# GpSimdE inverses, VectorE transposes of the small blocks, and two constant products ahead of each TensorE task of the first stage

## The chip, the cores and the metric

The kernel runs on one core of a Trainium2 chip. The metric is the device time of one execution in microseconds (us); a comparison uses medians of several runs. TensorE (PE in the profile) multiplies, VectorE (DVE), ScalarE (ACT) and GpSimdE (POOL) do elementwise work, and SyncE (SP) issues nearly all DMAs. TensorE's granted clock has two levels here, 1.2 and 2.4 GHz; the profile's PEclk gives their mean over a stretch, 0.5 and 1.0.

## The reference

A delta-rule attention over 4 batches, 8 heads, 768 steps and head size 48 feeds two feed-forward layers (width 384, hidden width 2048, 3072 tokens):

```python
for t in range(S):
    y[:, :, t] = q[:, :, t] @ state
    v_old = k_n[:, :, t] @ state
    state += beta[t] * outer(k_n[:, :, t], v[:, :, t] - v_old)
h = x @ w_in                       # first layer, rational function
P = a0 + a1*h + a2*h**2 + a3*h**3
Q = 1 + |b0|*|h| + |b1|*h**2
x = (P / (Q + 1e-6)) @ w_out
h = x @ w2_in                      # second layer
out = (max(h, 0)**2) @ w2_out
```

## The kernel before

The attention is cut into 12 chunks of 64 steps, and 4 batches of a chunk make 4 of its 48 sub-steps n (all heads at once). Within a chunk the recurrence is solved by the inverse of a triangular 64x64 matrix for each head, built from the Gram matrix of the keys. Eight sub-steps (two chunks) make a group g, of 0 to 5, whose inverses are made together.

**Inverses.** Tile Gb holds the 32x32 diagonal blocks of the Gram matrices, one block per partition, and Tt the inverses. For groups 2 to 5 the loop of L466 to L473 makes 31 steps of two VectorE operations each: a product into tmp (L471) and a subtraction into Tt (L472), of (s+1)(31-s) elements a partition (31 to 256), each depending on the one before. For groups 0 and 1 the loop of L457 to L465 inverts 16x16 blocks only, and products of TensorE on 32x32 blocks merge them: mA (L528) into E, mB (L540), mC (L552). For all groups m1 (L578) and m2 (L591) merge 32x32 blocks into 64x64 ones. ScalarE moves each result out of PSUM (L545, L557, L584, L596). Tt lies one block per partition, the products need blocks of rows: so Tt goes to DRAM (td) and comes back in four loads as TT, and its transpose (ScalarE's copy to Gb, L491) goes to DRAM (nd) and comes back as DN or TN.

**Sub-steps.** `first` computes K S and Q S (L666) and T v (also L666), `middle` copies and masks on ScalarE and GpSimdE (L699, L703), `rest` makes the outputs (L724, L725) and updates the state X on VectorE (L743). Outputs gather in xin, which `split` turns into xh and xl (L849, L850). Gram matrices of later groups (L425) go to DRAM in gs (L415).

**Feed-forward.** Layer 1 works in 6 tiles i of 512 tokens, each of 16 units j (128 hidden features): mm1 (9 products, L866) into a PSUM bank h, `rational` (L876 to L898), and mm2_1 (L904) some 15 us later. Tile i needs the two chunks of group i. Layer 2 follows with 96 units of mm1, relu2 and mm2_2 (L866, L915 to L930). There are three PSUM banks for h; a unit holds one until the last operation of `rational`, L895. In `rational` ScalarE copies h to SBUF (hs, L884), and GpSimdE makes b*a (L886), c = a3*hs + a2 (L887) and c*hs (L889).

**Order of work.** Nothing is ordered by hand. Every piece is a task with an engine, an estimated duration, a due time, and what it reads and writes; class Plan plays a list schedule of all tasks (`play`), moves due times by the result (`late`), repeats this 8 times and keeps the shortest. Each engine then executes its tasks strictly in that order, the DMAs of SP too. A task marked lock=1 on VectorE is never planned beside one marked so on GpSimdE. In `Plan.run`, gaps of over 0.6 us planned ahead of a TensorE task from 55 us before T0 = 88 us (planned start of layer 1) to 20 us after it are filled with products of a constant (128x128 by 128x256 bf16, L284), as many as 70% of the gap holds at 0.11 us each. They write a bank that is not read.

```python
for _ in range(int(0.7 * (gap - 0.2) / dur)):
    one()
```

## Time and profile before

| what | us |
|---|---|
| median of 3 runs | 1183.78 (1182.72 to 1186.74) |
| profiled execution, its own time | 1189.82 |
| its span, first to last instruction | 1188.1 |
| stage A, up to the first product of layer 1 | 113 |
| stage B, layer 1 with groups 1 to 5 of the attention | 113 to 785 |
| stage C, layer 2 | 785 to 1188 |

The page gives the busy time of each engine: PE 1088.5 us (92% of the span), DVE 716.0 (60%), ACT 676.3 (57%), POOL 459.2 (39%). These are means over three stages with different limits, so the profile is read by stage. In a row of the windows each engine has its busy time in us and, in brackets, its instructions. A row of the groups gives line, engine, operation, out<-in, shapes and count, then the busy time in us and the mean of one instruction in ns, then the idle time of the engine before them.

### The profile page before, as it was taken

The page shows a single profiled execution, that of the slowest core. Times are in us where ns is not written, and L with a number is a line of the kernel's source. Part 1 is how long each engine was busy: PE and PEld are TensorE (multiplying, and loading weights), DVE is VectorE, ACT ScalarE, POOL GpSimd, SP SyncE. Part 2 cuts the span into 40 slices and gives each one's busy share as a digit, 9 for nine tenths or more (in the row PEclk, how much of TensorE's full clock was granted, in tenths as well). Part 3 has the DMA queues.
Part 4 walks back from the last instruction along what each step waited for, and adds up shares of the span by engine and source line. Part 5 has one row for each costly group of instructions (what it writes and reads, how often), then busy time and mean ns, then how long its engine had stood idle before and what let it go on. Part 6 is the DMA issues. An engine that isn't in the chain of part 4 may idle for free.

```text
span 1188.1 us, 24846 instructions
## 1 busy us (share of the span) xinstructions
PE 1088.5 (92%) x10030; PEld 769.2 (65%) x10030; DVE 716.0 (60%) x1237; ACT 676.3 (57%) x1269; POOL 459.2 (39%) x479
## 2 busy tenths in 40 slices
PE   4687898799897998998899989999999999999998
PEld 4576565456554555655566646567788888888887
DVE  4353777887888689668755546788633343333432
ACT  5365876586667576765576867766523333243432
...
GB/s 223 175 186 162 85 65 144 142 152 40 84 80 126 15 86 87 109 9 59 54 81 17 20 83 80 33 154 138 67 9 27 27 18 36 1 27 1 27 1 27
DMA packets 135394, 87.83 MB, mean 74 GB/s; under 512 B 102384, under 2 KB 119920, under 8 KB 135280
## 3 DMA queue, kind: packets, MB, share of 16 engines
...
q14 instruction: 35, 0.29, 0.1%
...
## 4 chain that ended last, share of the span: by engine, by line
PE 72%; DVE 8%; issue 5%; DMA 4%; ACT 4%; POOL 3%; SPq 3%; ACTq 0%; POOLq 0%; DVEq 0%
PE bank L866 28%; PE bank L904 18%; PE bank L930 5%; PE bank L928 5%; PE bank L929 5%; PE bank L666 5%; SPq L316 3%; DVE tmp L471 2%; PE bank L724 2%; DVE Tt L472 2%; POOL A L825 1%; POOL C L832 1%; DMA kTg<-in_kS_dram 1%; DVE mem L893 1%; PE bank L578 1%
## 5 line engine op out<-in xcount | busy, mean ns | idle before, releaser
L866 PE MATMUL bank<-xh,A 128*128 128x512 f32 x1152 | 362.8, 396 | 3.6 <-POOL A L825 3.6
L904 PE MATMUL bank<-mem,B 128*128 128x512 f32 x576 | 289.0, 635 | 22.1 <-DVE mem L895 21.1
L866 PE MATMUL bank<-xl,A 128*128 128x512 f32 x576 | 258.7, 449 | 11.0 <-DVE mem L895 6.5
L866 PEld LDWEIGHTS bank<-xh,A 128*128 128x128 f32 x1152 | 219.9, 191 | 67.0 <-issue 15.1
L904 PEld LDWEIGHTS bank<-mem,B 128*128 128x128 f32 x576 | 107.6, 198 | 126.3 <-issue 88.7
L916 DVE SCALAR_TENSOR_TENSOR mem<-bank,mem 128x512 f32<-128x512 f32 x96 | 66.3, 691 | 152.2 <-ACT mem L915 152.1
L887 POOL TENSOR_SCALAR mem<-hs,par 128x512 f32<-128x512 f32 x96 | 79.6, 829 | 176.8 <-ACT hs L884 140.5
L866 PEld LDWEIGHTS bank<-xl,A 128*128 128x128 f32 x576 | 110.1, 191 | 54.3 <-issue 14.8
L915 ACT ACTIVATE mem<-bank 128x512 f32<-128x512 f32 x96 | 57.5, 599 | 152.2 <-PE bank L866 152.1
L886 POOL TENSOR_TENSOR mem<-mem 128x512 f32<-128x512 f32 x96 | 126.4, 1317 | 9.3 <-DVE mem L893 4.2
L889 POOL TENSOR_TENSOR mem<-mem,hs 128x512 f32<-128x512 f32 x96 | 125.4, 1306 | 7.4
L930 PE MATMUL bank<-gh,C 128*128 128x512 f32 x288 | 113.7, 395 | 0.0
L928 PE MATMUL bank<-gl,C 128*128 128x512 f32 x288 | 113.5, 394 | 0.0
L929 PE MATMUL bank<-gh,C 128*128 128x512 f32 x288 | 112.0, 389 | 0.0
L893 DVE SCALAR_TENSOR_TENSOR mem<-mem,par,bank 128x512 f32<-128x512 f32 x96 | 71.5, 745 | 61.0 <-ACT bank L892 60.6
L890 DVE SCALAR_TENSOR_TENSOR mem<-mem,par,bank 128x512 f32<-128x512 f32 x96 | 71.1, 741 | 59.4 <-POOL mem L889 56.0
L919 DVE TENSOR_TENSOR gl<-mem,gh 128x512 fp32r<-128x512 f32 x96 | 69.2, 722 | 60.0 <-ACT gh L918 60.0
L918 ACT CAST gh<-mem 128x512 fp32r<-128x512 f32 x96 | 59.6, 621 | 70.9 <-DVE mem L916 59.8
L883 ACT ACTIVATE mem<-bank 128x512 f32<-128x512 f32 x96 | 57.4, 598 | 73.2 <-PE bank L866 72.1
L891 ACT ACTIVATE mem<-mem,par 128x512 f32<-128x512 f32 x96 | 69.2, 721 | 29.2 <-POOL mem L886 28.5
L885 ACT ACTIVATE mem<-mem,par 128x512 f32<-128x512 f32 x96 | 78.5, 817 | 0.9
L703 POOL TENSOR_SCALAR_AFFINE_SELECT X<-X 64x256 f32<-64x256 f32 x96 | 42.0, 438 | 71.1 <-ACT X L699 64.4
(119 smaller groups left out, 1636.7 us busy)
## 6 DMA issues: line engine op xcount, KB each, us to landing
...
```

The lines of the kernel that those rows point to most:

```text
L866: M.matmul(h, a, b, start=(k == 0 and m == 0), stop=(k == NK - 1 and m == 2))
L885: add("ACT", 0.83, lambda: A_.activation(b(), a(), AF.Identity, bias=s(4), scale=s(5)), r=[ak, "par"], w=[bk], due=due + 3.8, alloc=(("b", ...
L886: add("POOL", 1.32, lambda: P_.tensor_tensor(b(), b(), a(), op=ALU.mult), r=[ak], w=[bk], due=due + 5, lock=1)
L887: add("POOL", 0.85, lambda: P_.tensor_scalar(c(), hs(), s(3), s(2), op0=ALU.mult, op1=ALU.add), r=[sk, "par"], w=[ck], due=due + 5, lock=1 ...
L889: add("POOL", 1.32, lambda: P_.tensor_tensor(c(), c(), hs(), op=ALU.mult), r=[sk], w=[ck], due=due + 6.5, lock=1, free=[sk])
L890: add("DVE", 0.775, lambda: V.scalar_tensor_tensor(c(), c(), s(1), h(), op0=ALU.add, op1=ALU.mult), r=[hk, "par"], w=[ck], due=due + 7.3)
L891: add("ACT", 0.72, lambda: A_.activation(a(), b(), AF.Ln, bias=s(6)), r=[bk, "par6"], w=[ak], due=due + 7)
L893: add("DVE", 0.775, lambda: V.scalar_tensor_tensor(c(), c(), s(0), h(), op0=ALU.add, op1=ALU.mult), r=[hk, "par"], w=[ck], due=due + 9)
L904: M.matmul(acc[d], Bw[j][:, 128 * d:128 * d + 128], slot[gk], start=(j == 0), stop=(j == NJ - 1))
L928: M.matmul(acc[d], wh, gl, start=(j == 0), stop=False)
L929: M.matmul(acc[d], wl, gh, start=False, stop=False)
L930: M.matmul(acc[d], wh, gh, start=False, stop=(j == NJ - 1))
```

## The change

Six edits come together. (1) The 31 inverse steps of groups 2 to 5 go from VectorE to GpSimdE. (2) `rational` drops the copy hs; c = a3*h + a2 is made by ScalarE out of PSUM, and h*c by VectorE. (3) For groups 0 and 1 two transposes on VectorE make Gb (the blocks of Tt, rows on partitions) and DN in place of the trips through td and nd; mA reads Gb instead of TT. (4) For group 0 the block N is made by ScalarE with a mask `half` instead of four DMAs; the copies `o2` go from ScalarE to VectorE. (5) `move`: for group 0, results at partitions 64 and above leave PSUM through VectorE, others through ScalarE as before, and each quarter is a task of its own. (6) Constant products: the window begins 64 us ahead of T0, gaps are filled by another formula, and each TensorE task planned from 58 us to 4 us ahead of T0 gets at least two. kTc has four buffers instead of three.

```diff
@@ -33,7 +33,7 @@
-ROUNDS = 8
+ROUNDS, FILL = 8, 2
...
-        lo, hi, one, dur = self.fill
+        lo, hi, one, dur, least = self.fill
         end = 0.0
         for i in self.order:
             if T[i]["eng"] == "PE":
                 gap = T[i]["s"] - max(end, lo)
-                if gap > 0.6 and T[i]["s"] < hi:
-                    for _ in range(int(0.7 * (gap - 0.2) / dur)):
-                        one()
+                n = int((gap - 0.2) / dur) if gap > 0.5 and T[i]["s"] < hi else 0
+                for _ in range(max(n, least if lo + 6 < T[i]["s"] < T0 - 4 else 0)):
+                    one()
                 end = T[i]["e"]
             T[i]["fn"]()
...
-    tiles(one, "hs", 2, [128, N])
-    PL.fill = (T0 - 55, T0 + 20, lambda: nc.tensor.matmul(banks[2][:, 0:N // 2], ones[:, 0:128], ones, start=True, stop=True), 0.11)
+    PL.fill = (T0 - 64, T0 + 20, lambda: nc.tensor.matmul(banks[2][:, 0:N // 2], ones[:, 0:128], ones, start=True, stop=True), 0.16, FILL)
-    tiles(at, "kTc", 3, [128, NP, C])
+    tiles(at, "kTc", 4, [128, NP, C])
...
+    def halves():
+        P_.memset(half, 1.0)
+        for o in range(0, 128, 32):
+            P_.affine_select(half[o:o + 32], half[o:o + 32], pattern=[[0, 1]], base=-16, channel_multiplier=1, compare_op=ALU.is_ge, fill=0.0)
+    add("POOL", 0.6, halves, w=["half"], due=5)
...
-                A_.copy(TN[o:o + 32, n], t[o:o + 32, :, 0:32])
+                V.tensor_copy(TN[o:o + 32, n], t[o:o + 32, :, 0:32])
-        add("ACT", 0.6, o2, r=[key], w=[("TN", 32), ("TN", 96)], due=n + 8, free=[key])
+        add("DVE", 0.6, o2, r=[key], w=[("TN", 32), ("TN", 96)], due=n + 8, free=[key])
...
+    def move(g, o, dur, get, f=None, **kw):
+
+        def act():
+            a, b = get()
+            A_.copy(a, b) if f is None else A_.mul(a, b, f)
+
+        def dve():
+            a, b = get()
+            V.tensor_copy(a, b) if f is None else V.tensor_scalar(a, b, f, None, op0=ALU.mult)
+        add(*(("DVE", dur, dve) if g == 0 and o >= 64 else ("ACT", dur, act)), **kw)
...
         for s in range(31 if g > 1 else 0):
             a, b = s + 1, 31 - s
 
-            def st(s=s, a=a, b=b):
+            def st1(s=s, a=a, b=b):
                 tv = tmp[:, :a * b].rearrange("p (a b) -> p a b", a=a)
-                V.tensor_tensor(tv, _mid(Gb[:, s, s + 1:32], [128, a, b]), Tt[:, 0:a, s:s + 1].to_broadcast([128, a, b]), op=ALU.mult)
-                V.tensor_tensor(Tt[:, 0:a, s + 1:32], Tt[:, 0:a, s + 1:32], tv, op=ALU.subtract)
-            add("DVE", 0.42 + 2.0e-3 * a * b, st, r=GB, w=["Tt", "tmp"], due=d1, lock=1)
-
-
-        if g < 2:
+                P_.tensor_tensor(tv, _mid(Gb[:, s, s + 1:32], [128, a, b]), Tt[:, 0:a, s:s + 1].to_broadcast([128, a, b]), op=ALU.mult)
+
+            def st2(s=s, a=a, b=b):
+                tv = tmp[:, :a * b].rearrange("p (a b) -> p a b", a=a)
+                P_.tensor_tensor(Tt[:, 0:a, s + 1:32], Tt[:, 0:a, s + 1:32], tv, op=ALU.subtract)
+            for st in (st1, st2):
+                add("POOL", 0.17 + 2.3e-3 * a * b, st, r=GB, w=["Tt", "tmp"], due=d1, lock=1)
+
+
+        if g == 0:
+            add("ACT", 0.85, lambda: A_.mul(Nb.rearrange("r s p c -> r (s p) c")[:, :, 0:16], Dg.rearrange("r s p c -> r (s p) c")[:, :, 0:16], half),
+                r=[("Dg", n) for n in range(8)] + ["half"], w=[("N", o) for o in range(0, 128, 32)], due=d1)
+        elif g == 1:
...
-        dma(512, td[g], Tt, r=["Tt"], w=[("td", g)], due=d1, lat=2.0)
-        add("ACT", 2.05, lambda: A_.copy(Gb, Tt.rearrange("p a b -> p b a")), r=["Tt"], w=GB, due=d1)
+        if g < 2:
+            add("DVE", 2.0, lambda: V.transpose(Gb.rearrange("r q c -> r c q"), Tt.rearrange("p a b -> p b a")), r=["Tt"], w=GB, due=d1, lock=1)
+            add("DVE", 2.0, lambda: V.transpose(DN.rearrange("r s p c -> r c (s p)"), Tt), r=["Tt"], w=["DN"], due=d1 + 1, lock=1)
+        else:
+            dma(512, td[g], Tt, r=["Tt"], w=[("td", g)], due=d1, lat=2.0)
+            add("ACT", 2.05, lambda: A_.copy(Gb, Tt.rearrange("p a b -> p b a")), r=["Tt"], w=GB, due=d1)
...
-        for i in (1, 0):
+        for i in (1, 0) if g > 1 else ():
-        if g < 2:
-            sk = add("ACT", 0.4, lambda: A_.dma_start(nd[g], Gb), r=GB, due=d1)
-            add("LAND", 4.0, lambda: None, r=GB, w=[("nd", g)], due=d1 + 2, after=[sk])
-            ndv = nd[g].rearrange("(o q) r c -> o r q c", o=4)
-            for o in (32, 96, 0, 64):
-                dma(128, DN[o:o + 32].rearrange("r s p c -> r (s p) c"), ndv[o // 32], r=[("nd", g)], w=[("DN", o)], due=d1 + 3, lat=3.4, iss=0.6)
-        else:
+        if g > 1:
...
                         for o in range(0, 128, 32):
-                            M.matmul(w[o:o + 32, s, p], Nb[o:o + 32, 4 * hf + s, p], TTg[o:o + 32, 4 * hf + s, p, o % 64:o % 64 + 32],
-                                     start=True, stop=True)
+                            M.matmul(w[o:o + 32, s, p], Nb[o:o + 32, 4 * hf + s, p], Gb[o:o + 32, 16 * hf + 4 * s + p], start=True, stop=True)
...
-            def mbo(hf=hf):
+            def mbo(o, hf=hf):
                 t = ps(("mB", g, hf), [128, 4, NP, 32])
-                for o in (32, 96, 0, 64):
-                    A_.copy(TTg[o:o + 32, 4 * hf:4 * hf + 4, :, o % 64:o % 64 + 32], t[o:o + 32])
+                return TTg[o:o + 32, 4 * hf:4 * hf + 4, :, o % 64:o % 64 + 32], t[o:o + 32]
...
+            add("PE", 2.4, ma, r=nn + GB, w=[ka], due=dd, alloc=(pl, ka), free=["merge"])
             add("DVE", 0.8, me, r=[ka, "ident"], w=["E"], due=dd, free=[ka, "merge"])
-            add("PE", 2.4, mb, r=["E"] + dn_, w=[kb], due=dd, alloc=(pl, kb), free=["merge"])
-            add("ACT", 2.4, mbo, r=[kb] + tx, w=[("TD", g, hf)], due=dd, free=[kb])
-            add("PE", 1.3, mc, r=["E"] + dn_, w=[kc], due=dd, alloc=(pl, kc), free=["merge"])
-            add("ACT", 1.2, mco, r=[kc], w=[("TNh", hf, 0), ("TNh", hf, 1)], due=dd, free=[kc])
+            add("PE", 2.4, mb, r=["E", "DN"], w=[kb], due=dd, alloc=(pl, kb), free=["merge"])
+            for o in (32, 96, 0, 64):
+                move(g, o, 0.6, lambda o=o, f=mbo: f(o), r=[kb], w=[("TD", g, hf, o)], due=dd, free=[kb], after=[PL.last[wT[0]]])
+            add("PE", 1.3, mc, r=["E", "DN"], w=[kc], due=dd, alloc=(pl, kc), free=["merge"])
+            for o in (0, 64):
+                move(g, o, 0.6, lambda o=o, f=mco: f(o), r=[kc], w=[("TNh", hf, o // 64)], due=dd, free=[kc])
...
+            td_ = [("TD", g, hf, o) for o in range(0, 128, 32)] if g < 2 else []
+            add("PE", 1.3, m1, r=g21 + [("TTx", g % 2, 1, 0), ("TTx", g % 2, 1, 1)] + td_, w=[kw], due=dd, alloc=(pl, kw))
+            for o in (0, 64):
+                move(g, o, 0.6, lambda o=o, f=m1o: f(o), -1.0, r=[kw], w=[("ws", o)], due=dd, free=[kw])
+            add("PE", 1.3, m2, r=[("TN", 0), ("TN", 64), ("TNh", hf, 0), ("TNh", hf, 1), ("ws", 0), ("ws", 64)], w=[kt_], due=dd, alloc=(pl, kt_))
+            for o in (0, 64):
+                move(g, o, 0.6, lambda o=o, f=m2o: f(o), r=[kt_], w=[("T", g % 2, hf, o)], due=dd, free=[kt_],
+                     after=[PL.last["TTx", g % 2, 0, x] for x in range(2)] if g > 1 else [PL.last[wT[0]]])
...
-        add("ACT", 0.62, lambda: A_.copy(hs(), h()), r=[hk], w=[sk], due=due + 3, alloc=(("hs",), sk))
-        add("ACT", 0.83, lambda: A_.activation(b(), a(), AF.Identity, bias=s(4), scale=s(5)), r=[ak, "par"], w=[bk], due=due + 3.8, alloc=(("b",), bk))
-        add("POOL", 1.32, lambda: P_.tensor_tensor(b(), b(), a(), op=ALU.mult), r=[ak], w=[bk], due=due + 5, lock=1)
-        add("POOL", 0.85, lambda: P_.tensor_scalar(c(), hs(), s(3), s(2), op0=ALU.mult, op1=ALU.add), r=[sk, "par"], w=[ck], due=due + 5, lock=1,
-            alloc=(("c",), ck))
-        add("POOL", 1.32, lambda: P_.tensor_tensor(c(), c(), hs(), op=ALU.mult), r=[sk], w=[ck], due=due + 6.5, lock=1, free=[sk])
-        add("DVE", 0.775, lambda: V.scalar_tensor_tensor(c(), c(), s(1), h(), op0=ALU.add, op1=ALU.mult), r=[hk, "par"], w=[ck], due=due + 7.3)
-        add("ACT", 0.72, lambda: A_.activation(a(), b(), AF.Ln, bias=s(6)), r=[bk, "par6"], w=[ak], due=due + 7)
-        add("ACT", 0.62, lambda: A_.activation(h(), a(), AF.Exp, scale=-1.0), r=[ak], w=[hk], due=due + 8, free=[ak])
-        add("DVE", 0.775, lambda: V.scalar_tensor_tensor(c(), c(), s(0), h(), op0=ALU.add, op1=ALU.mult), r=[hk, "par"], w=[ck], due=due + 9)
-        add("DVE", 0.72, lambda: V.scalar_tensor_tensor(h(), b(), 1.0 + EPS, h(), op0=ALU.add, op1=ALU.mult), r=[bk], w=[hk], due=due + 9.8, free=[bk])
-        add("DVE", 0.72, lambda: V.scalar_tensor_tensor(g(), h(), -2.0, c(), op0=ALU.add, op1=ALU.mult), r=[hk, ck], w=[gk], due=due + 10.6,
+        add("ACT", 0.83, lambda: A_.activation(b(), a(), AF.Identity, bias=s(4), scale=s(5)), r=[ak, "par"], w=[bk], due=due + 3.3, alloc=(("b",), bk))
+        add("ACT", 0.79, lambda: A_.activation(c(), h(), AF.Identity, bias=s(2), scale=s(3)), r=[hk, "par"], w=[ck], due=due + 4.5, alloc=(("c",), ck))
+        add("POOL", 1.32, lambda: P_.tensor_tensor(b(), b(), a(), op=ALU.mult), r=[ak], w=[bk], due=due + 4.2, lock=1)
+        add("DVE", 0.69, lambda: V.tensor_tensor(c(), h(), c(), op=ALU.mult), r=[hk], w=[ck], due=due + 5.5)
+        add("DVE", 0.75, lambda: V.scalar_tensor_tensor(c(), c(), s(1), h(), op0=ALU.add, op1=ALU.mult), r=[hk, "par"], w=[ck], due=due + 6.3)
+        add("ACT", 0.72, lambda: A_.activation(a(), b(), AF.Ln, bias=s(6)), r=[bk, "par6"], w=[ak], due=due + 6)
+        add("ACT", 0.62, lambda: A_.activation(h(), a(), AF.Exp, scale=-1.0), r=[ak], w=[hk], due=due + 7, free=[ak])
+        add("DVE", 0.75, lambda: V.scalar_tensor_tensor(c(), c(), s(0), h(), op0=ALU.add, op1=ALU.mult), r=[hk, "par"], w=[ck], due=due + 8)
+        add("DVE", 0.7, lambda: V.scalar_tensor_tensor(h(), b(), 1.0 + EPS, h(), op0=ALU.add, op1=ALU.mult), r=[bk], w=[hk], due=due + 8.8, free=[bk])
+        add("DVE", 0.7, lambda: V.scalar_tensor_tensor(g(), h(), -2.0, c(), op0=ALU.add, op1=ALU.mult), r=[hk, ck], w=[gk], due=due + 9.6,
```

## Rows read from the trace of the kernel before

**Rows 1.** Windows by stage; stage B by tile i; columns: start:end, length, engines, PEclk, DMA

```profile
0.00:113.00 113.00, 76.30 (x1999) 65.92 (x1999) 51.37 (x136) 58.14 (x134) 32.35 (x60) 0.70 0.69 184
113.00:253.00 140.00, 119.16 (x1910) 77.60 (x1909) 103.68 (x193) 96.07 (x182) 74.30 (x74) 0.90 0.46 125
253.00:367.00 114.00, 104.21 (x1015) 63.02 (x1014) 94.25 (x169) 78.38 (x154) 67.95 (x70) 0.97 0.29 79
367.00:486.00 119.00, 109.12 (x1265) 67.08 (x1263) 95.31 (x170) 78.52 (x155) 66.73 (x68) 0.94 0.35 80
486.00:596.00 110.00, 100.28 (x878) 61.50 (x875) 80.69 (x158) 71.48 (x139) 60.55 (x63) 0.95 0.18 51
596.00:701.00 105.00, 103.95 (x1005) 63.73 (x1004) 59.16 (x99) 77.29 (x149) 61.79 (x65) 1.00 0.17 37
701.00:785.00 84.00, 77.45 (x243) 46.13 (x242) 56.14 (x78) 60.30 (x97) 59.28 (x52) 0.98 0.22 75
785.00:1188.00 403.00, 397.99 (x1730) 324.26 (x1728) 175.39 (x239) 156.11 (x263) 36.29 (x28) 1.00 0.11 38
```

**Rows 2.** Waits of PE, 300 to 400 us; columns: us in total, times, longest

```profile
PE bank L904 <- DVE mem L895: 8.9, 5, 3.4
```

**Rows 3.** Groups of instructions by line, whole span, DVE, POOL and ACT

```profile
L472 DVE TENSOR_TENSOR Tt<-Tt,tmp 128x31 f32<-128x31 f32 (+15 forms) x124 | 63.0, 508 | 4.3
L471 DVE TENSOR_TENSOR tmp<-Gb,Tt 128x31 f32<-128x31 f32 (+15 forms) x124 | 62.8, 506 | 1.9
...
L886 POOL TENSOR_TENSOR mem<-mem 128x512 f32<-128x512 f32 x96 | 126.4, 1317 | 9.3 <-DVE mem L893 4.2 <-ACT mem L885 3.1 <-DVE nT L454 1.4
L889 POOL TENSOR_TENSOR mem<-mem,hs 128x512 f32<-128x512 f32 x96 | 125.4, 1306 | 7.4
L887 POOL TENSOR_SCALAR mem<-hs,par 128x512 f32<-128x512 f32 x96 | 79.6, 829 | 176.8 <-ACT hs L884 140.5 <-issue 34.5 <-POOL X L703 0.9
...
L336 POOL TENSOR_SCALAR_AFFINE_SELECT ident<-ident 32x32 f32<-32x32 f32 x4 | 0.8, 206 | 0.2
...
L885 ACT ACTIVATE mem<-mem,par 128x512 f32<-128x512 f32 x96 | 78.5, 817 | 0.9
...
L884 ACT COPY hs<-bank 128x512 f32<-128x512 f32 x96 | 56.0, 584 | 12.2 <-PE bank L866 11.8
...
L894 DVE SCALAR_TENSOR_TENSOR bank<-mem,bank 128x512 f32<-128x512 f32 x96 | 66.1, 688 | 0.0
```

**Rows 4.** Groups by form, DVE: small inverse steps of groups 0 and 1

```profile
L464 DVE TENSOR_TENSOR Tt<-Tt,tmp 128x30 f32<-128x30 f32 x4 | 0.8, 201 | 0.1
...
L464 DVE TENSOR_TENSOR Tt<-Tt,tmp 128x128 f32<-128x128 f32 x2 | 0.6, 292 | 0.1
```

**Rows 5.** Source line L471: duration ns min/median/max, first and last start

```profile
L471 DVE TENSOR_TENSOR tmp<-Gb,Tt x124: 179/404/1508, 145.6 to 593.1; 128x31 f32<-128x31 f32 x8, 128x60 f32<-128x60 f32 x8, 128x87 f32<-128x87 f32 x8, 128x112 f32<-128x112 f32 x8
```

**Rows 6.** Timeline of stage A: start us, length us, instruction, idle before and releaser

```profile
15.23 1.94 DVE L435 STREAM_TRANSPOSE Gb<-TT 128x1024 f32<-128x1024 f32 x1
...
29.75 0.21 DVE L464 TENSOR_TENSOR Tt<-Tt,tmp 128x30 f32<-128x30 f32 x1
...
43.27 2.64 PE L528 MATMUL bank<-TT,mem 32*32 32x32 f32 x239
...
54.74 0.48 PE L540 MATMUL bank<-mem,DN 32*32 32x32 f32 x18 [4.09 <-issue]
...
66.10 2.37 ACT L545 COPY TT<-bank 32x512 f32<-32x512 f32 x4 [3.60 <-PE bank L540]
...
72.43 1.95 PE L666 MATMUL bank<-vn,TT 64*64 64x48 f32 x32
...
107.69 3.81 PE L284 MATMUL bank<-ones 128*128 128x256 bf16 x17
...
112.96 0.50 PE L866 MATMUL bank<-xl,A 128*128 128x512 f32 x1
```

**Rows 7.** Waits of the SP queue, 0 to 113 us

```profile
SPq L316 <- DMA nd<-Gb: 6.1, 1, 6.1
```

**Rows 8.** Window 72 to 80 us, columns as in rows 1

```profile
72.00:80.00 8.00, 8.00 (x175) 7.06 (x175) 0.76 (x3) 4.65 (x11) 0.00 (x0) 0.50 0.79 226
```

37 lines of the change are left out of this document (14 added, 23 removed).

## The prediction

> **What bounds the kernel now.** I read the profile in this order: windows by stage, waits of TensorE, groups of VectorE and GpSimdE, then the timeline of the first stage.
>
> The windows [rows 1] show three stages. In stage C TensorE is busy 398 of 403 us at full clock; nothing there is touched, and I cost it at nothing. In stage B each line is one tile of 16 units. Tile 4 is the measure: 105 us with TensorE busy 104 and the clock at 1.00. It holds attention work, but no inverse step: the last one of L471 starts at 593.1 us [rows 5]. Tiles 0 to 3, which hold one inverse chain each, take 140, 114, 119 and 110 us. TensorE is idle in them for 21, 10, 10 and 10 us, and the granted clock is down to 0.90 to 0.97. VectorE is what is full: 94 of 114 us in tile 1, against 59 of 105 in tile 4. The wait that ends last there is the next product L904 for VectorE's last operation of a unit, L895 [rows 2]. So in tiles 1 to 3 VectorE is the bound and TensorE idles behind it; in tile 0, which also converts all weights of the layer, both VectorE (104) and ScalarE (96 of 140) are well loaded.
>
> In stage A (113 us) no engine is full; TensorE is busy 76 us at a mean clock of 0.70 [rows 1]. It is a chain of latencies: the inverse of group 0 is finished at 29.96 us, mA starts at 43.27, T v at 72.43, layer 1 at 112.96 [rows 6].
>
> **The inverse steps, VectorE to GpSimdE.** VectorE loses L471 and L472: 125.8 us in four groups, 31.4 us a tile [rows 3]. These steps are dearer than they need be: the median of L471 is 404 ns and the longest 1508 [rows 5], while 128 elements take 292 ns and 30 elements 201 in groups 0 and 1 [rows 4]. From those two, a step costs 0.173 us and 0.93 ns an element; 62 steps with 2 x 5456 elements would be 10.7 + 10.1 = 20.9 us.
>
> On GpSimdE no row shows such a step (short rows, a spread operand). The nearest is L886, two inputs, 1317 ns for 512 elements, with 206 ns of L336 for a small operation [rows 3]: 2.17 ns an element. That gives 62 x 0.206 + 10912 x 0.00217 = 12.8 + 23.7 = 36.5 us a group, which I take. From below, L887 with one input (829 ns) gives 1.22 ns an element and 26 us; from above, every step at the whole 1317 ns gives 82 us. GpSimdE has room: in tile 4 it is busy 61.8 us, of which L887 and L889 take 16 x 2.135 = 34.2 and go. 27.6 + 36.5 = 64 of 105 us. The wait added is of L886, queued behind a step on GpSimdE; a step of 256 elements would hold it 0.8 us, less than L887 and L889, which follow it now.
>
> The Trainium skill, page GPSIMD Engine Reference, section on performance versus the Vector engine, speaks against this edit: a two-input elementwise operation is about twice as slow on GpSimdE (1.96 times in its measurement). Of the clear price that would be 41 us instead of 36.5, which alters nothing; of the price VectorE really pays (507 ns a step) it would be 62, and that is a rival below.
>
> **The rational function.** Per unit GpSimdE loses 829 + 1306 ns; ScalarE changes a copy of 584 for an operation like L885, 817: +0.23; VectorE gains a product with one operand in PSUM, as L894: +0.69 [rows 3]. Per tile that is GpSimdE -34, ScalarE +3.7, VectorE +11.0. VectorE in tile 1 comes to 94 - 31.4 + 11.0 = 74 us, ScalarE to 82, TensorE to 104 less some 3 us that go when the clock is full. TensorE becomes the bound, as in tile 4. The two new operations lie in a unit's chain, but beside b*a on GpSimdE, 1317 ns; if that cover goes they cost up to 1.5 us of latency a unit, which three banks for h hide as long as TensorE has other work.
>
> **Sum of stage B.** Tiles 1 to 3 come to the 105 us of tile 4: -9, -14, -5, together -28; they hold Gram products for later groups that tile 4 lacks, so I take -24. Bounds: nothing, if ScalarE's and SP's order takes VectorE's place, and -35, if only TensorE's work at full clock is left. Tile 0: 21 us idle and 0.10 x 140 = 14 us of slow clock are to be had; ScalarE stays at 100 us and the weights still pass VectorE, so I take half, -18 (bounds 0 and -34). Tile 5 loses 34 us of GpSimdE and gains 11 of VectorE (67 of 84): 0, bounds -5 and +5. Together -42.
>
> **Stage A, the trips through DRAM.** From 29.96 to 43.27 us is 13.3 us. In its place stands one transpose ahead of mA, 1.94 us as L435 [rows 6], the second beside mA: -11 (bounds -9, with both transposes ahead, and -13). SP loses for each of groups 0 and 1 one store and eight loads, for group 0 also four loads for N; the queue stood 6.1 us for nd [rows 7], with the query loads of the second chunk behind it. I take -3 of it (0 to -6). For group 1 the same trip ran beside layer 1's start; its products can now run earlier, which I count as nothing (0 to -5 in tile 0).
>
> **Small moves.** Halving ScalarE's four moves of mB (2.37 us [rows 6]) and those after it saves 2 us on the chain of group 0 (0 to -5). The copies o2 on VectorE and the mask on GpSimdE cost nothing: VectorE's first transpose starts only at 15.23. If that cover goes, 16 copies of PSUM cost VectorE some 4 us. The stalls marked issue, such as the 4.09 us in L540, stay.
>
> **The constant products.** At the low clock one takes 3.81 / 17 = 0.22 us [rows 6]. I count some 50 tasks of TensorE in the window, so 100 products, 22 us, against about 37 us of idle time in the stage [rows 1]; some replace gap products already there. On the other side the clock is 0.50 in 72 to 80 us although TensorE is busy all 8.00 us with small products [rows 8]; with full-size products between, the chain there might run at the upper level. Whether two a task suffice no row shows. From above +11, from below -11 (half of 22 us of such work); I take 0.
>
> **Sum.** Stage A -11 - 3 - 2 = -16, stage B -42: -58 us. Against the profiled execution, 1189.8 - 58 = 1131.8; that execution lies 6.0 us over the median of the runs, so the median becomes 1183.8 - 58, about **1126 us**.
>
> **Rivals.** *Something else takes VectorE's place.* ScalarE carries the moves of the attention, the weights and one more long operation a unit, all in a planned order, and could be what is late in tiles 0 to 3. Then stage B gives 6 us and stage A 16: 1162. For it, ScalarE's 100 us in tile 0; against it, tile 4, where ScalarE is busy 77 us and delays nothing. Chance 0.19.
>
> *GpSimdE's chain ends as late as VectorE's did.* At 62 us a chain, twice the 507 ns a step [rows 3], GpSimdE is busy 90 of 105 us in a tile; the chain with the work between fills its 80 to 90 us as now, and tiles 1 to 3 give nothing: 1126 + 24 = 1150. This is what the skill's factor gives on the price paid; the rows of L886 speak for less. Chance 0.14.
>
> *Slower: the steps are far dearer on GpSimdE.* Each step has rows of 1 to 31 elements, and no row shows what such a shape costs there. A tile ends no sooner than 27.6 us plus the chain, since the attention of the next group waits for it. Tiles 0 to 3 take 121 us on average, so it decides from a chain of 93 us, 1.5 us a step. At 1.7 us a step the chain is 105, four tiles last 133 each, 47 us more, less the 16 of stage A: 1215. That is over twice the price by L886, hence 0.09.
>
> *The gains cancel.* The plan is remade and constant products stand in the way where TensorE was free: about 1184, chance 0.04.
>
> **How the numbers follow.** The forecast has 0.54, with 1090 to 1148 as its own bounds. The range is 1085 to 1172: below, stage A at -30 and tiles at their floors (-70) give -100; above, stage A alone at -12. It leaves out the two last rivals and some of the tails. A measurement of this kernel can tell about 0.3% (3.6 us) from no change. Faster: forecast and the first two rivals, 0.87; same 0.04; slower 0.09.
>
> **What would show it.** Right: L471 and L472's successors on GpSimdE at about 0.6 us each; tiles 0 to 3 with TensorE busy over 95% and VectorE under 75%; the first product of layer 1 at 92 to 102 us; mA within 4 us of the last small inverse step; stage C unchanged at 403 us. Wrong: steps over 1 us on GpSimdE with TensorE waiting for products of the attention; waits of L904 for L895 that stay; ScalarE over 90% in tiles 1 to 3; a first stage that is still over 108 us because SP or a weight load is late.

## The result, and the profile after

| what | before, same chip | after |
|---|---|---|
| median, us | 1184.92 | 1144.39 (1142.65 to 1145.55) |
| ratio to before, 95% interval | | 0.9658 [0.9633, 0.9682] |
| profiled execution, its own time, us | 1189.82 | 1143.41 |
| its span, us | 1188.1 | 1141.7 |

The change saves 3.4%: faster, as forecast, and the 1144 us lie within the range; the point forecast of 1126 was 18 us too low. In the profiled executions the saving is 46.4 us of the 58 forecast, 11.6 short. The other 7 us of the miss are the step from execution to median: the execution before lay 6 us over the median I started from, 1183.78, the one after lies 1 us under its own.

Of the kernel after, windows by stage and tile, same columns as [rows 1] (busy us and count of PE, PEld, DVE, ACT, POOL, then clock, DMA share, GB/s):

```profile
0.00:104.00 104.00, 83.91 (x2275) 64.66 (x2275) 63.09 (x150) 42.67 (x102) 28.81 (x59) 0.79 0.58 166
104.00:249.00 145.00, 124.63 (x1840) 82.70 (x1828) 102.53 (x168) 101.66 (x189) 87.99 (x114) 0.92 0.42 117
249.00:354.00 105.00, 101.18 (x1123) 63.03 (x1121) 72.88 (x124) 82.81 (x155) 64.05 (x96) 0.98 0.37 91
354.00:457.00 103.00, 101.65 (x1138) 63.28 (x1136) 68.62 (x118) 83.83 (x157) 62.45 (x97) 0.99 0.37 90
457.00:557.00 100.00, 99.15 (x1008) 62.12 (x1007) 66.55 (x116) 77.83 (x142) 60.99 (x96) 1.00 0.24 61
557.00:659.00 102.00, 101.47 (x830) 61.70 (x829) 67.36 (x112) 77.96 (x144) 27.28 (x33) 1.00 0.09 28
659.00:741.00 82.00, 76.74 (x243) 46.14 (x241) 67.42 (x98) 65.80 (x104) 31.83 (x26) 0.98 0.26 90
741.00:1141.70 400.70, 397.11 (x1730) 324.28 (x1728) 166.80 (x234) 152.38 (x256) 25.52 (x22) 1.00 0.10 35
```

Tiles 1 to 3 are what the change is worth: 105, 103 and 100 us where [rows 1] had 114, 119 and 110, TensorE busy 96 to 99% of them, VectorE 67 to 69% instead of 73 to 83%. Stage A is 9 us shorter, not 16. Tile 0, for which 18 us less were forecast, is 5 us longer.

The waits of PE from 250 to 350 us, columns as in [rows 2]. The wait for VectorE's last operation of a unit is gone; one late ScalarE operation is all that is left:

```profile
PE bank L923 <- ACT mem L904: 3.8, 1, 3.8
```

The groups that answer to [rows 3]: the two inverse steps (L492, L488), b*a (L907), c (L906), h*c (L908):

```profile
L907 POOL TENSOR_TENSOR mem<-mem 128x512 f32<-128x512 f32 x96 | 123.3, 1285 | 209.9 <-ACT mem L905 209.3
...
L906 ACT ACTIVATE mem<-bank,par 128x512 f32<-128x512 f32 x96 | 73.6, 769 | 0.7
...
L492 POOL TENSOR_TENSOR Tt<-Tt,tmp 128x31 f32<-128x31 f32 (+15 forms) x124 | 70.8, 571 | 8.5
...
L488 POOL TENSOR_TENSOR tmp<-Gb,Tt 128x31 f32<-128x31 f32 (+15 forms) x124 | 66.0, 532 | 19.6 <-DVE Tt L473 11.5
...
L908 DVE TENSOR_TENSOR mem<-bank,mem 128x512 f32<-128x512 f32 x96 | 65.8, 686 | 58.4 <-ACT mem L906 58.2
```

An inverse step takes 0.55 us on GpSimdE; a group's 62 take 34.2 us (36.5 forecast).

The timeline of stage A, against [rows 6]: last small inverse step, two transposes, mA, T v, first product of layer 1.

```profile
29.85 0.21 DVE L481 TENSOR_TENSOR Tt<-Tt,tmp 128x30 f32<-128x30 f32 x1
...
30.09 2.08 DVE L514 STREAM_TRANSPOSE Gb<-Tt 128x1024 f32<-128x1024 f32 x1
...
32.04 1.93 DVE L515 STREAM_TRANSPOSE DN<-Tt 128x1024 f32<-128x1024 f32 x1
...
32.32 0.86 PE L549 MATMUL bank<-Gb,mem 32*32 32x32 f32 x80
...
59.58 0.88 PE L686 MATMUL bank<-vn,TT 64*64 64x48 f32 x12
...
104.18 0.48 PE L887 MATMUL bank<-xl,A 128*128 128x512 f32 x1
```

mA starts 11.0 us earlier than before and T v 12.9; but from T v to layer 1 it now takes 44.6 us, where it was 40.5. In tile 0 the third unit starts at 110 us and the fourth at 143 (before: 118 and 132). This wait of the units is called the hole below. The timeline of ScalarE, VectorE and TensorE in it:

```profile
119.16 1.75 ACT L429 COPY TT<-bank 32x512 f32<-32x512 f32 x3
...
120.94 2.12 ACT L906 ACTIVATE mem<-bank,par 128x512 f32<-128x512 f32 x3
...
121.82 0.69 DVE L908 TENSOR_TENSOR mem<-bank,mem 128x512 f32<-128x512 f32 x1 [8.28 <-ACT mem L906]
...
135.40 0.84 DVE L836 SCALAR_TENSOR_TENSOR B<-mem 128x384 uint32<-128x384 uint32 x1
136.17 1.87 DVE L914 SCALAR_TENSOR_TENSOR mem<-bank,mem 128x512 f32<-128x512 f32 x3
...
138.82 5.35 PE L923 MATMUL bank<-mem,B 128*128 128x512 f32 x6
...
143.32 1.08 PE L887 MATMUL bank<-xl,A 128*128 128x512 f32 x1
```

The three c of the first units (L906) stand in ScalarE's planned order behind group 1's moves (L429), and VectorE idles 8.3 us for them. The hole ends with the last operation of `rational` of the three units (L914), which frees their banks of h. VectorE runs it right behind a copy of unit 3's weights (L836): in the kernel these weights lie in the buffers g that L914 writes.

At the tile's other end, the timeline of TensorE, GpSimdE and VectorE ahead of group 1's last two sub-steps:

```profile
212.72 0.98 PE L686 MATMUL bank<-X,kTc 48*64 48x112 f32 x16
...
218.40 1.27 POOL L907 TENSOR_TENSOR mem<-mem 128x512 f32<-128x512 f32 x1 [3.82 <-ACT mem L905]
...
221.60 1.01 POOL L492 TENSOR_TENSOR Tt<-Tt,tmp 128x31 f32<-128x31 f32 x1
222.56 1.47 POOL L641 TENSOR_TENSOR vn<-vn,nT 128x768 f32<-128x768 f32 x1
...
224.38 0.34 DVE L729 TENSOR_TENSOR vn<-vn,bank 128x192 f32<-128x192 f32 x1
...
230.21 0.32 PE L686 MATMUL bank<-vn,TT 64*64 64x48 f32 x4
```

The 16 products at 212.72 us are K S and Q S of the first sub-step of group 2, which the plan puts ahead of group 1's last two sub-steps. They fill one of the two PSUM banks that the kernel keeps for attention, until VectorE has subtracted K S from the v of the next chunk (L729). GpSimdE has to scale that v first (L641), in its queue behind the last inverse step of group 2 (L492), which itself stands behind a b*a that waited for ScalarE. The last two T v follow, at 230 and 232 us; the one before them was at 205.

### The profile page after: what moved, and what is told of

The parts are those of the page before. It is cut to its first block, busy times and chain, and to the rows that moved or that the text cites. A ratio compares the mean times of both kernels' runs of the same rounds, so it can differ in the third digit from the quotient of the medians.

```text
span 1141.7 us, 24884 instructions
## 1 busy us (share of the span) xinstructions
PE 1085.8 (95%) x10162; PEld 767.9 (67%) x10162; DVE 675.2 (59%) x1115; ACT 684.9 (60%) x1242; POOL 388.9 (34%) x540
## 4 chain that ended last, share of the span: by engine, by line
PE 88%; ACT 4%; DVE 3%; DMA 2%; issue 2%; SPq 1%; POOL 0%; DVEq 0%; ACTq 0%
PE bank L887 34%; PE bank L923 22%; PE bank L686 6%; PE bank L949 6%; PE bank L947 6%; PE bank L948 6%; PE bank L745 2%; PE bank L283 2%; PE bank L597 1%; PE bank L609 1%; DMA kTg<-in_kS_dram 1%; DMA vn<-in_vn_dram 1%; PE bank L442 1%; SPq L316 1%; ACT mem L905 1%
## 5 line engine op out<-in xcount | busy, mean ns | idle before, releaser
L923 PE MATMUL bank<-mem,B 128*128 128x512 f32 x576 | 282.8, 621 | 6.5 <-ACT mem L904 3.8
L907 POOL TENSOR_TENSOR mem<-mem 128x512 f32<-128x512 f32 x96 | 123.3, 1285 | 209.9 <-ACT mem L905 209.3
L923 PEld LDWEIGHTS bank<-mem,B 128*128 128x128 f32 x576 | 104.9, 193 | 100.9 <-issue 79.9
L935 DVE SCALAR_TENSOR_TENSOR mem<-bank,mem 128x512 f32<-128x512 f32 x96 | 66.2, 690 | 156.9 <-ACT mem L934 156.9
L887 PEld LDWEIGHTS bank<-xl,A 128*128 128x128 f32 x576 | 109.1, 189 | 47.3 <-issue 15.9
L912 DVE SCALAR_TENSOR_TENSOR mem<-mem,par,bank 128x512 f32<-128x512 f32 x96 | 71.4, 743 | 69.0 <-ACT bank L911 68.7
L908 DVE TENSOR_TENSOR mem<-bank,mem 128x512 f32<-128x512 f32 x96 | 65.8, 686 | 58.4 <-ACT mem L906 58.2
L906 ACT ACTIVATE mem<-bank,par 128x512 f32<-128x512 f32 x96 | 73.6, 769 | 0.7
L492 POOL TENSOR_TENSOR Tt<-Tt,tmp 128x31 f32<-128x31 f32 (+15 forms) x124 | 70.8, 571 | 8.5
```

Of the source, the lines that this page charges most:

```text
L492: P_.tensor_tensor(Tt[:, 0:a, s + 1:32], Tt[:, 0:a, s + 1:32], tv, op=ALU.subtract)
L887: M.matmul(h, a, b, start=(k == 0 and m == 0), stop=(k == NK - 1 and m == 2))
L906: add("ACT", 0.79, lambda: A_.activation(c(), h(), AF.Identity, bias=s(2), scale=s(3)), r=[hk, "par"], w=[ck], due=due + 4.5, alloc=(("c", ...
L907: add("POOL", 1.32, lambda: P_.tensor_tensor(b(), b(), a(), op=ALU.mult), r=[ak], w=[bk], due=due + 4.2, lock=1)
L912: add("DVE", 0.75, lambda: V.scalar_tensor_tensor(c(), c(), s(0), h(), op0=ALU.add, op1=ALU.mult), r=[hk, "par"], w=[ck], due=due + 8)
L923: M.matmul(acc[d], Bw[j][:, 128 * d:128 * d + 128], slot[gk], start=(j == 0), stop=(j == NJ - 1))
```

## The experiments

Stage A here ends with the first product of layer 1, and a tile lasts from its first product to the next tile's. "Last sub-step" is the start of group 1's last T v. All times in us, of the profiled execution; the ratio is to the kernel before on the same chip.

| kernel | stage A | tile 0 | tiles 1 to 3 | last sub-step | tile 1 starts | ratio |
|---|---|---|---|---|---|---|
| before | 113.0 | 139.9 | 114.3, 118.8, 110.5 | 212 | 253 | 1 |
| after | 104.2 | 144.8 | 104.7, 103.2, 100.6 | 232 | 249 | 0.9658 |
| e1 | 103.3 | 156.9 | 117.5, 109.9, 110.3 | 249 | 260 | 0.9974 |
| e2 | 103.5 | 178.0 | 113.9, 111.3, 111.8 | 269 | 282 | 1.0183 |
| e3 | 107.5 | 129.2 | 102.9, 100.6, 100.2 | 224 | 237 | 0.9494 |
| e4 | 93.1 | 144.6 | 101.2, 100.4, 100.1 | 221 | 238 | 0.9500 |
| e5 | 96.2 | 145.1 | 101.0, 100.4, 100.0 | 224 | 241 | 0.9535 |
| e6 | 95.5 | 159.4 | 104.7, 101.3, 100.5 | 241 | 255 | 0.9665 |
| e7 | 93.3 | 151.7 | 98.8, 100.4, 100.2 | 228 | 245 | 0.9550 |
| e8 | 94.7 | 151.7 | 100.6, 99.9, 99.3 | 232 | 246 | 0.9564 |
| e9 | 94.9 | 138.8 | 102.4, 101.0, 100.1 | 196 | 234 | 0.9490 |
| e10 | 94.0 | 137.7 | 103.0, 104.9, 96.9 | 193 | 232 | 0.9460 |
| e11 | 99.0 | 161.4 | 114.2, 116.7, 108.8 | 217 | 260 | 1.0007 |
| e12 | 109.1 | 130.5 | 101.0, 101.5, 98.9 | 199 | 240 | 0.9509 |

Two orders in time hold over these runs; "L729" and the like stand for the same operation at whatever line a run has it. In the nine kernels where the first products of group 2 stand ahead of group 1's last two sub-steps (after, e1 to e8), the first of the two starts 2 to 7 us after L729 has ended, wherever that is, from 213 to 262 us. In the other five (before, e9 to e12) the products stand behind them, and the last sub-step starts by 217 us. And in the eleven kernels with the edits of the first stage the hole is 25 to 37 us long, and in all but e7 VectorE starts L914 as the copy of unit 3's weights (L836) ends, from 123 to 143 us. In the other three (before, e3, e12) that copy runs at 105 to 109 us and the hole is 14 us. No run moved the products or the copy by itself, so that they are the cause is likely, but not shown.

### e1: the inverse back on VectorE

```diff
-                P_.tensor_tensor(tv, ...)
+                V.tensor_tensor(tv, ...)
...
-                P_.tensor_tensor(Tt[:, 0:a, s + 1:32], ...)
+                V.tensor_tensor(Tt[:, 0:a, s + 1:32], ...)
...
-            add("POOL", 0.17 + 2.3e-3 * a * b, st, ...)
+            add("DVE", 0.42 + 2.0e-3 * a * b, st, ...)
```

> The changed kernel with the 31 inverse steps of groups 2 to 5 back on VectorE, all else as changed. Theory (VectorE's load bounds tiles 0 to 3): VectorE gets 31 us a tile back and keeps the 11 us of the new product, 73 + 31 = 104 us in a tile that takes 105 now, so tiles 1 to 3 go to 112 to 125 us each and the whole to 1170 to 1205 us. Rival (the gain came from GpSimdE losing L887 and L889, not from VectorE): tiles 1 to 3 stay within 4 us of 105, 103 and 100, the whole within 10 us of 1144.

Measured: 1185.17 us, ratio 0.9974 [0.9944, 1.0005]: without this edit nothing is left of the gain. Its tile 1 (columns as above):

```profile
260.20:377.70 117.50, 104.09 (x1131) 65.32 (x1131) 88.99 (x179) 81.22 (x154) 30.75 (x34) 0.94 0.32 75
```

the longest wait of TensorE from 260 to 360 us, again for VectorE's last operation of a unit:

```profile
PE bank L919 <- DVE mem L910: 4.9, 2, 4.0
```

and its groups of the inverse, now on VectorE:

```profile
L489 DVE TENSOR_TENSOR Tt<-Tt,tmp 128x31 f32<-128x31 f32 (+15 forms) x124 | 46.6, 376 | 4.2
L488 DVE TENSOR_TENSOR tmp<-Gb,Tt 128x31 f32<-128x31 f32 (+15 forms) x124 | 44.8, 361 | 1.6
```

VectorE is at 89 of 117 us (94 of 114 before the change [rows 1]), although its steps got cheaper: 91.4 us in all instead of 125.8 [rows 3], with the same operations on the same data. What went is GpSimdE's two other operations a unit. The timeline of the kernel before shows the mechanism on one pair of steps of the same size, the first beside a GpSimdE product, the second just after its end at 294.15:

```profile
292.86 1.29 POOL L886 TENSOR_TENSOR mem<-mem 128x512 f32<-128x512 f32 x1
...
293.60 0.74 DVE L471 TENSOR_TENSOR tmp<-Gb,Tt 128x175 f32<-128x175 f32 x1
...
294.38 0.34 DVE L472 TENSOR_TENSOR Tt<-Tt,tmp 128x175 f32<-128x175 f32 x1
```

Of the 248 steps before, 45 lay mostly beside one of GpSimdE's two-input operations and took 1108 ns on average. Against steps of the same size and kind beside which GpSimdE was idle (taken here, in e1 and in e11) that is slow: at their mean, the 45 would take 345 ns, and all 248 together 84 us instead of 126. A third of what the inverse cost VectorE was so lost beside GpSimdE, 34 of the 42 us in those 45 steps.

### e2: the rational function as before

```diff
-        add("ACT", 0.79, ... c(), h(), AF.Identity, bias=s(2), scale=s(3)) ...
-        add("DVE", 0.69, ... V.tensor_tensor(c(), h(), c(), op=ALU.mult)) ...
+        add("ACT", 0.62, ... A_.copy(hs(), h())) ...
+        add("POOL", 0.85, ... P_.tensor_scalar(c(), hs(), s(3), s(2), ...)) ...
+        add("POOL", 1.32, ... P_.tensor_tensor(c(), c(), hs(), op=ALU.mult)) ...
...
-    tiles(at, "kTc", 4, [128, NP, C])
+    tiles(at, "kTc", 3, [128, NP, C])
```

> The changed kernel with the rational function as before (copy hs, two more operations on GpSimdE, none on VectorE) and three kTc buffers. Theory: VectorE falls by 11 us a tile, GpSimdE rises by 34 to some 97 of 105 us and its inverse chain, queued among the longer operations, ends late: tiles 0 to 3 go to 110 to 120 us, the whole to 1160 to 1200. Rival (the rational part is worth nothing by itself): within 6 us of 1144.

Measured: 1209.11 us, ratio 1.0183 [1.0145, 1.0221], dearer than expected. Tiles 0 and 1 (columns as above):

```profile
103.50:281.50 178.00, 138.37 (x1949) 90.10 (x1947) 101.95 (x160) 100.26 (x192) 122.73 (x146) 0.84 0.35 99
281.50:395.40 113.90, 102.39 (x1134) 64.07 (x1131) 59.48 (x102) 78.41 (x155) 93.82 (x129) 0.96 0.36 85
```

and the longest of TensorE's waits in tile 0 (us in total, times, longest), for weights that ScalarE and GpSimdE prepare:

```profile
PE bank L888 <- ACT A L846: 10.5, 3, 4.2
```

GpSimdE has both loads here (94 of 114 us in tile 1), VectorE is nearly free at 59, and the tile is as long as before. Moving the inverse alone seems only to move the bound; that it lies on GpSimdE now is read from this load, since TensorE's own waits in tile 1 are spread (at most 3.2 us for any one operation). It takes both edits: each alone, with the edits of the first stage, leaves tiles 1 to 3 at 338 (e1) and 337 us (e2), where they had 344 before and 309 after. The sum on record gave the two one gain between them, which is the right way to count.

### e3: only these two, without the edits of the first stage

The kernel before, with the inverse on GpSimdE, the new rational function and the fourth kTc buffer.

```diff
-    tiles(at, "kTc", 3, [128, NP, C])
+    tiles(at, "kTc", 4, [128, NP, C])
...
-            add("DVE", 0.42 + 2.0e-3 * a * b, st, ...)
+            for st in (st1, st2):
+                add("POOL", 0.17 + 2.3e-3 * a * b, st, ...)
...
```

> The kernel before with two parts of the change alone: inverse steps on GpSimdE and the new rational function; DRAM trips, moves and constant products as before. Theory: stage A stays at 111 to 115 us, tiles 1 to 3 come to 100 to 106 each as in the changed kernel, the whole to 1145 to 1160. On tile 0: if its stall of the changed kernel (no layer-1 product from 112 to 143 us) comes from group 1's products being ready early and pulled in among the first units, tile 0 takes 118 to 130 us here; if it comes from ScalarE's new operation standing late in its order, it takes 138 to 150 here too.

Measured: 1127.37 us, ratio 0.9494 [0.9458, 0.9530]. Half of the change beats the whole by 1.7%, and comes out 18 us under the range expected. Stage A and tile 0:

```profile
0.00:107.50 107.50, 69.18 (x1994) 59.94 (x1994) 56.91 (x135) 57.99 (x134) 34.17 (x57) 0.74 0.72 193
107.50:236.70 129.20, 114.94 (x1974) 74.22 (x1972) 89.59 (x150) 97.38 (x180) 76.53 (x108) 0.95 0.47 124
```

Tile 0 is 129 us and its hole 14, so what it lost belongs to the edits of the first stage; tile 1 starts at 237 us. Stage A is 5.5 us shorter than before though none of its own edits is in; the plan is remade for the whole kernel, and which of its shifts does this was not tried.

### e4: no two products ahead of each task

```diff
-ROUNDS, FILL = 8, 2
+ROUNDS, FILL = 8, 0
```

> The changed kernel with no least number of constant products ahead of a task (gap products stay); the plan is the same. Theory (two products a task cost some 0.45 us each time at the low clock and do not lift it from 41 to 72 us): the first layer-1 product comes at 97 to 101 us instead of 104.4, the whole 3 to 7 us under 1144. Rival (they lift the clock after 72 us and before 41 us): the first product comes at 106 to 112 us, the whole 2 to 8 us over 1144.

Measured: 1127.67 us, ratio 0.9500 [0.9459, 0.9542]; first layer-1 product at 93.1 us, tile 1 at 238. The planned order of all else is the same, so the two a task cost 11 us in stage A and 17 in all, more than the theory had. The other 7 us of the spans lie in tiles 1 to 3, where no constant product runs any more; why is not shown. The group of the constant products in the kernel after:

```profile
L283 PE MATMUL bank<-ones 128*128 128x256 bf16 x210 | 36.6, 298 | 0.5 <-issue 0.5
```

and in this run:

```profile
L283 PE MATMUL bank<-ones 128*128 128x256 bf16 x124 | 19.0, 312 | 0.0
```

86 products and 17.6 us of busy time less. They didn't lift the clock where it was low. The window of that stretch (columns as above) in the kernel before:

```profile
51.00:82.00 31.00, 23.23 (x688) 20.94 (x689) 16.34 (x51) 18.42 (x37) 0.00 (x0) 0.51 0.61 187
```

in the kernel after:

```profile
42.00:72.00 30.00, 26.56 (x641) 19.91 (x638) 11.51 (x26) 10.45 (x22) 2.30 (x4) 0.50 0.46 114
```

and in this run:

```profile
37.00:68.00 31.00, 24.22 (x910) 22.78 (x910) 15.19 (x31) 11.43 (x25) 7.67 (x11) 0.51 0.52 128
```

It is 31 us long in all three and only moves forward with the merges of group 0, and the constant products in it are 12, 27 and none. Of the 11 us, 10 come after T v: from there to layer 1 it takes 34.4 us here and 44.6 in the kernel after, with 21 constant products (3.0 us busy) here and 85 (17.3 us) there.

This run beside e3 is the other half of the answer on tile 0. Layer 1 starts 14 us earlier than in e3, and tile 1 starts at the same time, 238 and 237 us.

### e5: no constant products at all

(on e4)

```diff
-                n = int((gap - 0.2) / dur) if gap > 0.5 and T[i]["s"] < hi else 0
+                n = 0
```

> The changed kernel without any constant products: not the two ahead of each task, nor those that fill the gaps of the plan (124 of them in the run without the two a task, 1127.67 us); the planned order of all other work is that of that run. Theory (gap products only cost TensorE time, as the two a task did: in the run before, 23 of them, 4.3 us, stand on the chain of waits at 112 to 116 us, ahead of a merge that was ready): first layer-1 product at 90 to 93 us, tile 0 at 139 to 144 us, total 1117 to 1125. Rival (they hold the clock up between the merges): longer stretches at the low level in stage A, first layer-1 product at 95 to 100 us, total 1129 to 1137.

Measured: 1130.21 us, ratio 0.9535 [0.9513, 0.9557]; first layer-1 product at 96.2 us. Neither theory holds cleanly: stage A is 3 us longer than in e4, as the rival said, its clock 0.72, and TensorE runs at the lower level from 111 to 135 us where e4 had 112 to 115 and 122 to 132. The two intervals overlap, and the runs were on different chips, so the gap products are worth some 3 us if anything; the two a task cost several times that.

### e6: group 1's merges behind the first units

```diff
-            add("PE", 2.4, ma, r=nn + GB, ..., free=["merge"])
+            add("PE", 2.4, ma, r=nn + GB, ..., free=["merge"], nb=T0 + 40 if g else 0.0)
```

(on e4, as are the next four)

> The changed kernel without the two constant products a task (1127.67 us), with the merges of group 1 put behind the first units of tile 0 in the plan. Theory (the 33 us without a unit in tile 0 come from group 1's merges, which hold ScalarE, VectorE and TensorE between the third and the fourth unit): the gap falls to 14 to 22 us (before the change it was 14), tile 0 is 5 to 12 us shorter, total 1116 to 1123. Rival (tile 0's end is set by group 1's sub-steps, not by its units): the gap falls all the same, but the first sub-step of group 1 comes 10 to 25 us later than 156 us and tile 0 is as long or longer, 144 to 158 us, total 1127 to 1141.

Measured: 1146.71 us, ratio 0.9665 [0.9648, 0.9683]. The hole between third and fourth unit falls from 33 to 25 us, not to 14 to 22, and 5 of these 8 us only because the third unit starts later: the merges explain a small part. The rival's other half came true and more: group 1's first sub-step starts at 177 us instead of 156, tile 0 lasts 159. What the units win at the start of the tile doesn't reach its end.

### e7: half of group 1's moves on VectorE

```diff
-        add(*(("DVE", dur, dve) if g == 0 and o >= 64 else ("ACT", dur, act)), **kw)
+        add(*(("DVE", dur, dve) if g < 2 and o >= 64 else ("ACT", dur, act)), **kw)
```

> The changed kernel without the two constant products a task (1127.67 us), with half of group 1's moves out of PSUM on VectorE, as group 0's are. Theory (ScalarE's queue holds the first units: c of three units stands behind four moves): the gap between third and fourth unit falls from 33 to 26 to 30 us, tile 0 is 3 to 6 us shorter, total 1121 to 1125. Rival (VectorE and the order of the merges hold them as much): gap and tile 0 within 2 us of 33 and 144.6, total 1126 to 1131.

Measured: 1132.86 us, ratio 0.9550 [0.9527, 0.9574]; the hole is 37 us, tile 0 151.7. Worse than either said; VectorE, with the moves added, ends the copy of unit 3's weights at 130 us instead of 126. ScalarE's queue is not by itself the cause.

### e8: the 32-row inverses due 20 us later

```diff
-STEP0, STEP1, INV0, INV1 = 40, 25, -90, -10
+STEP0, STEP1, INV0, INV1 = 40, 25, -70, -10
```

> The changed kernel without the two constant products a task (1127.67 us), with every 32-row inverse due 20 us later. Theory (the last two sub-steps of group 1 wait behind the end of group 2's inverse on GpSimdE's queue: their masks stand behind steps that end at 210 us): the inverse of group 2 runs some 10 to 20 us later, those two sub-steps move with it from 219 us to 226 to 238 us, tile 0 is 6 to 15 us longer, total 1131 to 1143. Rival (they wait for something else, and the inverse among the first units is what costs): the two sub-steps come at 210 to 220 us, tile 0 is 2 to 8 us shorter, total 1119 to 1126.

Measured: 1132.90 us, ratio 0.9564 [0.9544, 0.9584]. The outcome is the theory's: group 2's inverse ends at 218 us instead of 211, the last two sub-steps start at 230 and 232 instead of 219 and 221, tile 1 at 246 instead of 238. What stands behind the inverse in GpSimdE's queue is not their masks, as the theory had it, but the scaling of the next chunk's v (at 219 us instead of 211); L729, which reads it, follows at 222 instead of 213.

### e9 and e10: sub-steps due 10 and 20 us earlier

```diff
-STEP0, STEP1, INV0, INV1 = 40, 25, -90, -10
+STEP0, STEP1, INV0, INV1 = 30, 35, -90, -10
```

and in e10

```diff
-STEP0, STEP1, INV0, INV1 = 40, 25, -90, -10
+STEP0, STEP1, INV0, INV1 = 20, 45, -90, -10
```

> The changed kernel without the two constant products a task (1127.67 us), with the sub-steps of every group from group 1 on due 10 us earlier in the plan. Theory (the end of tile 0 is set by group 1's sub-steps, in every run so far some 14 to 17 us after the last of them began, 221 us here and 238 us for tile 1): the last sub-step of group 1 begins at 195 to 212 us, tile 1 at 222 to 231 us, tile 0 is 6 to 16 us shorter, total 1111 to 1121. Rival (units, not sub-steps, end tile 0, and sub-steps put first only take their place): the sub-steps come earlier, but tile 1 starts at 235 us or later, 14 us rule broken, total 1124 to 1135.

> As the run with sub-steps due 10 us earlier, here 20 us. Theory: once the last sub-step of group 1 begins at 190 to 206 us, the units of tile 0 set its end instead (16 units at 5 to 6 us behind the stall that ends at 132 us, with mean 6 us: 222 to 230 us), so this gains at most 3 us more than the other, total 1109 to 1120. Rival (units pushed back by the earlier sub-steps): tile 1 starts later than in the run with 10 us, total 2 to 8 us above it.

Measured: e9 1125.75 us, ratio 0.9490 [0.9454, 0.9527]; e10 1122.28 us, ratio 0.9460 [0.9424, 0.9496], the lowest median ratio of the study, though its interval overlaps those of e3, e4 and e9. In e9 the last sub-step comes 25 us earlier, at 196 us, but tile 1 only 4, at 234; in e10 193 and 232. Tile 1 at 234 us lies between e9's theory (222 to 231) and its rival (235 or later), and e10 misses its theory's total by 2 us. Half right: with the sub-steps late, tile 1 follows the last of them by 11 to 17 us (after and e1 to e8); with them early, by 38 to 41 (e9, e10, e12), as it did before the change (41). Then the units end the tile, and they allow only 4 to 6 us more. Tile 0 of e9, with VectorE busy 111 of 139 us where the kernel after had 103 of 145:

```profile
94.90:233.70 138.80, 123.33 (x1965) 82.14 (x1963) 111.27 (x173) 101.64 (x189) 87.05 (x113) 0.93 0.46 125
```

### e11 and e12: each half of the change once more

e11 is the edits of the first stage alone, without the two products a task; e12 is e3 with the due times of e9.

e11, beside the edits of e1 and e2:

```diff
-ROUNDS, FILL = 8, 2
+ROUNDS, FILL = 8, 0
```

e12, beside those of e3:

```diff
-STEP0, STEP1, INV0, INV1 = 40, 25, -90, -10
+STEP0, STEP1, INV0, INV1 = 30, 35, -90, -10
```

> Only the edits of the first stage (transposes, Nb on ScalarE, moves split, TN copies on VectorE), without the two constant products a task; the 32-row inverse on VectorE and the rational function as before the change. Theory (what stage A gains is given back in tile 0, since group 1's first sub-step comes at 156 to 162 us and tile 0's end follows from there, however early the first unit starts): first layer-1 product at 92 to 96 us, tile 1 not before 245 us, tiles 1 to 3 as before at 110 to 119 us each, total 1172 to 1189. Rival (stage A's 18 us stay): tile 1 starts at 231 to 238 us, total 1163 to 1171.

> The kernel before with the second half of the change alone (32-row inverse on GpSimdE, new rational function; 1127.37 us) and the sub-steps due 10 us earlier: the pair of the run with the whole change, no two products a task and the same due times (1125.75 us). Theory (stage A's end is worth nothing where tile 0 is set by what comes after): first layer-1 product at 105 to 110 us, last sub-step of group 1 at 190 to 205 us, tile 1 at 228 to 237 us, total 1117 to 1127. Rival (with the sub-steps out of the way stage A counts): tile 1 at 241 to 249 us, total 1131 to 1139.

Measured: e11 1189.42 us, ratio 1.0007 [0.9973, 1.0041]; e12 1128.46 us, ratio 0.9509 [0.9473, 0.9545]. e11: stage A is 14 us shorter and tile 0 21 us longer, with VectorE busy 122 us of it:

```profile
0.00:99.00 99.00, 73.27 (x2060) 64.87 (x2061) 61.45 (x144) 41.98 (x100) 26.71 (x58) 0.67 0.59 167
99.00:260.40 161.40, 132.00 (x1954) 86.14 (x1951) 121.94 (x218) 98.81 (x190) 83.64 (x81) 0.87 0.43 114
```

So a shorter first stage is worth nothing by itself here. The theory's reason is not the one at work: group 1's first sub-step starts at 138 us and the last 43 us ahead of tile 1, so it is the units that end the tile, as before the change. e12 starts layer 1 at 109 us and tile 1 at 240, e9 at 95 and 234: of 14 us, 6 are left at the next tile and 4 in the span (1123.0 against 1126.9), and the ratios' intervals overlap. Both outcomes lie just past the theory's edge, far from the rival's in e11, between the two in e12.

## Why the prediction was right, and where it failed

**Right: what bounds tiles 1 to 3, and the price on GpSimdE.** VectorE's load was the bound; e1 puts it back and the 10 us a tile come back with it. The step cost 0.55 us where 0.588 was worked out from L886 and L336. GpSimdE's inverses of groups 3 to 5 end 56 us after they began, where VectorE's took 88 to 93, so the rival of a chain as late as VectorE's falls, and that of 1.5 us a step with it; only group 2's, in tile 0, spreads over 93 us (90 before) between operations that wait. The Trainium skill, page GPSIMD Engine Reference, section on performance versus the Vector engine, gave 1.96; against VectorE's undisturbed steps of the same sizes (340 ns) the ratio here is 1.62, against what VectorE really paid (507) it is 1.09, and the lower one decided.

**Undersized: tiles 1 to 3.** The term "come to the 105 us of tile 4", -24, measured -35, its lower bound. 105 us was no floor: tile 4 itself fell to 102, with 175 products fewer in it (1005 before, 830 after) and TensorE busy 101.47 us instead of 103.95. Tiles 4 and 5 and stage C, taken as 0, gave -3, -2 and -2.

**Failed: tile 0, -18 by "I take half".** It was +5, outside its bounds of 0 and -34. The step asked for TensorE's idle time, its clock and which engine was full, not for the order of the work and the buffers that it holds. What sets the tile's end after the change is a second chain, group 1's sub-steps, all of which must be done before tile 1: the last began 41 us ahead of tile 1 before the change and 17 us after it. The last two follow group 2's first products and L729, which frees their bank. With the inverse on GpSimdE, the scaling of v that L729 reads stands in GpSimdE's queue behind the last inverse step: moving the inverse moves the two sub-steps (e8), putting the sub-steps first takes the wait away (e9, e10). The inverse is not the only way to it: in e1, which has no inverse step on GpSimdE, they start at 246 and 249 us, because VectorE comes to the subtraction in its own order only at 243. I had seen GpSimdE's queue, and priced it for b*a held by a step; that the steps are held in turn by a b*a that waits for ScalarE, and pass this on to what stands behind them, I had not.

Behind that bound lies a second one 4 to 6 us away, the units, whose hole at the tile's start grew from 14 to 33 us. That "the weights still pass VectorE" was in the step as load alone; that a copy of weights holds the buffers of the first units was not. The rival "something else takes VectorE's place" named ScalarE's order; it came true in this tile alone, and with VectorE's and GpSimdE's orders. What makes the hole is shown in part only: group 1's merges are at most 8 us of it (e6), ScalarE's moves by themselves none (e7), and that the copy of weights sets its end is read from the times of all runs, not tried.

**Failed: the constant products, taken as 0.** They cost 11 us in stage A (e4), the upper bound, with 86 products added where I had counted 100. "Two a task might hold the upper level" was the gain set against it, and no run shows one: the stretch at the lower level is as long with them as without.

**Right: the trips through DRAM**, -11: mA starts 2.5 us after the last small step and 11.0 earlier than before. With the products away stage A is 20 us shorter than before (e4), and 14 where the second half is left out too (e11); 16 were forecast without them. Tile 0 gives most or all of it back (e4 against e3, e11).

In spans: stage A -8.8 (-16), tile 0 +4.9 (-18), tiles 1 to 3 -35.1 (-24), the rest -7.5 (0): -46.5 instead of -58. The sum is nearer than its terms by luck: stage A and tile 0 fell 30 us short, the other parts gave 19 us more. Two of the signs set for being right did not come: the first product of layer 1 at 104.2 us (92 to 102), and TensorE busy 86% of tile 0 (over 95%).
